# Two staging slots in turn for the split weights of a second product, a slot of its own for the last result of the first MLP, and the split weights reloaded in quarters

## The chip, the cores and the metric

One NeuronCore of a Trainium2 chip runs the whole program. The metric is device time in microseconds (us) of one launch. Three runs of the kernel before gave 925.35, 929.89 and 929.4 us, median 929.4. The profile is of one further execution, 927.71 us, with a span of 926.0 us from its first to its last instruction; the 1.71 us around it are outside the trace.

## The reference

Attention with a causal window of 128 and a linear bias, then two MLPs on 2304 tokens, all in float32:

```python
scores = np.where(mask, scale * q @ k.T + bias, -1e9)      # 4 x 8 heads, 576 tokens, 64 wide
x = softmax(scores) @ v                                    # as 2304 x 512
h = x @ w_in;  x = np.where(h > 0, h, np.exp(np.minimum(h, 0)) - 1) @ w_out     # 512 -> 2048 -> 512
h = x @ w_in2; out = np.maximum(0.01 * h, h) @ w_out2                           # 512 -> 2048 -> 512
```

## The kernel before

Every float32 factor of a matmul is split into a rounded part and its remainder (`hi` by a copy on ScalarE, ACT; `lo` by a subtraction on VectorE, DVE), and each product is three matmuls: hi hi, hi lo, lo hi (`split_mm`).

The first MLP runs over five blocks of tokens `BLK1`, J = 0 to 4, and inside a block over 16 chunks c of 128 hidden units: `mlp1_h` (12 matmuls), activation, and two chunks later `mlp1_y` (12 matmuls) into four PSUM banks y0 to y3. After the last chunk the banks are copied to a tile `ys`, and from there stored to `x2T` in HBM. For J = 4 that is one tile `all_ys` for all four banks.

The second MLP is computed as a 2 x 2 block product with seven products instead of eight. The weights' block sums were made earlier and lie in HBM (`s_in` and `s_out`). Its first half, the 24 units `unit(u)` in three groups of 768 tokens, splits the sums of w_in2 as it goes (`s_load` brings 1,024 KB per pair p into slots w0 to w7, `split_w` splits them). A unit issues its products in the order 1, 5, 4, 6, 3, 2, 7, six matmuls each, where 4 and 3 belong to the unit before; it makes four results, c11, c22, c21 and c12. c11, c22 and c12 lie in turn in three buffers `eg`, c21 and the copy `a` in three buffers `gl`, and `g2_out` stores each to `g2T` in HBM. So c11 of unit u + 1 is written where c11 of unit u was, once its store has landed. The bank of product 2, `pw`, is y0 for an even unit and y1 for an odd one, so unit 0's product 2 waits until y0 has been copied to `ys`.

Its second half, `second(n)`, is 3 x 28 steps of 12 matmuls on results read back from g2T (`raw_load`) and on split weights read from `hlT` (`hl_load`, two tiles of 1,024 KB for each product m).

`hlT` is filled during the 16 chunks of J = 4, one step per chunk: `four_load(n)` reads 512 KB from `s_out` into one of two buffers `wf`, `four_split(n)` splits them with one instruction on ACT (line 301) and one on DVE (line 302) into a tile `hl` of 1,024 KB, and stores that to hlT (line 303). All 16 tiles `hl`, and then `all_ys`, have the one slot "wraw". In the same chunks `s_load` brings the eight tiles s, `x2_load` the first MLP's result for a group (`xr`), and `x2_job` makes the operands of the first products from it.

What sets the order: each engine executes its own queue in order, and so does SyncE's queue (SP), which issues nearly all DMAs. Matmuls, and a few other instructions, are pinned in program order by `keep_in_program_order`; the rest is placed by a list scheduler at build time. A slot of a pool is reused when the last reader of its old tile is done, and a DMA is such a reader until it has landed.

Of the kernel before, what the change touches and what calls it, by code (L numbers as in the profile page):

```python
# [10 lines left out]
F32 = mybir.dt.float32  # L11
F32R = mybir.dt.float32r
# [10 lines left out]
P = 128  # L23
NPAIR = H // 2
NK = DM // P
# [8 lines left out]
HALF = GRP // 2  # L34
NG = NT // GRP
NP2 = NC // 2
# [62 lines left out]
def attention_elu_leaky_kernel(  # L99
# [13 lines left out]
    nc = tc.nc  # L113
# [25 lines left out]
    wp = ctx.enter_context(tc.tile_pool(name="w", bufs=1))  # L139
    wrawp = ctx.enter_context(tc.tile_pool(name="wraw", bufs=1))  # L140
# [116 lines left out]
    hlT = dram.tile([P, 2, 8, NP2, 2 * P], F32, name="hlT")  # L257
# [39 lines left out]
    def four_split(n):  # L297

        src = FOURS.pop(n)
        t = wrawp.tile([P, 2, 4, 2 * P], F32R, tag="wraw", name="hl")  # L300
        nc.scalar.copy(t[:, 0], src)  # L301
        nc.vector.tensor_tensor(t[:, 1], src, t[:, 0].bitcast(F32), op=ALU.subtract)  # L302
        nc.sync.dma_start(out=hlT[:, :, n % 2 * 4:n % 2 * 4 + 4, n // 2], in_=t.bitcast(F32))
# [292 lines left out]
    def mlp1_y(J, cs, gg):  # L596
        gh, gl = gg
        t0, n = BLK1[J]
        per = 512 // n
        if cs[0] == 0:  # L600
            Y[J] = [psp.tile([P, per, n], F32, tag=f"y{i}", name=f"y{i}") for i in range(NK // per)]
        for ci, i, m in [(ci, i, m) for ci in range(len(cs)) for i in range(3) for m in range(NK)]:
            woh, wol = weights(1, cs[ci], 1)
            w, g = ((woh, gh), (woh, gl), (wol, gh))[i]

            matmul(Y[J][m // per][:, m % per, :], w[:, m * P:(m + 1) * P], g[:, ci * n:ci * n + n],
                             start=cs[ci] == 0 and i == 0 and m % per == 0, stop=cs[ci] == NC - 1 and i == 2,
                             skip_group_check=True)
        if cs[-1] == NC - 1:
            if J == len(BLK1) - 1:  # L610

                all_ys = wrawp.tile([P, NK, n], F32, tag="wraw", name="ys")
            for i, y in enumerate(Y.pop(J)):
                if J == len(BLK1) - 1:
                    ys = all_ys[:, i * per:i * per + per]
                else:
                    ys = egp.tile([P, per, n], F32, tag="eg", name="ys")
                if i % 2:
                    nc.vector.tensor_copy(ys, y)  # L619
                else:  # L620
                    nc.scalar.copy(ys, y)  # L621

                q = nc.sync if J < len(BLK1) - 2 or i % 2 else nc.scalar
                q.dma_start(out=x2T[:, i * per:i * per + per, t0:t0 + n], in_=ys)
# [75 lines left out]
    for J in range(len(BLK1) - 1):  # L700
        t0, n = BLK1[J + 1]
# [39 lines left out]
    def s_load(p):  # L741
        t = wp.tile([P, 8, 2 * P], F32, tag=f"w{p}", name="s")
        for o, i, n in ((0, 4, 3), (3, 0, 4), (7, 7, 1)):
            nc.sync.dma_start(out=t[:, o:o + n], in_=sT["in"][:, p, i:i + n])
        S["in", p] = t

    def split_w(u, part):

        s = S["in", u % NP2]
        if part == 2:  # L750
            t = wfp.tile([P, 2, 2, 2 * P], F32R, tag="wf", name="h2")
            hi, lo = t[:, 0], t[:, 1]
            cuts = [(0, 2, 6)]
            H2[u] = hi, lo
        else:
            hi = wp.tile([P, 5, 2 * P], F32R, tag=f"w{8 + u % 2 * 2}", name="h1")
            lo = wp.tile([P, 5, 2 * P], F32R, tag=f"w{9 + u % 2 * 2}", name="l1")
            cuts = [(3, 5, 0), (0, 3, 0)]
            H1[u] = hi, lo
        for a, b, o in cuts:  # L760
            nc.scalar.copy(hi[:, a:b], s[:, a + o:b + o])  # L761
            nc.vector.tensor_tensor(lo[:, a:b], s[:, a + o:b + o], hi[:, a:b].bitcast(F32), op=ALU.subtract)
# [46 lines left out]
        elif n == 6:  # L809
            split("b22", b(1, 1))  # L810

    ps2 = {}

    def product(m, u, bank, start):
        g = u // NP2
        xh, xl = OP[g, OP_OF[m]]
        i = W_OF[m]
        wh, wl = (x[:, i - 6] for x in H2[u]) if i > 5 else (x[:, i] for x in H1[u])
        for kk in range(2):
            s = slice(kk * P, (kk + 1) * P)  # L820
            split_mm(bank, wh[:, s], wl[:, s], xh[:, kk, :], xl[:, kk, :], start and kk == 0, kk == 1,
                     skip_group_check=True)

    def g2_out(u, c, half, tile_, src):
        g, p = divmod(u, NP2)
        nc.scalar.activation(tile_, src, AF.Prelu, alpha=0.01)
        t0 = g * GRP + half * HALF
        nc.sync.dma_start(out=g2T[:, 2 * p + c, t0:t0 + HALF], in_=tile_)

    def small(home, tag, name):  # L830
        return home.tile([P, HALF], F32, tag=tag, name=name)
# [46 lines left out]
    def raw_load(g, role, q, cell):  # L878
        j, k = int(role[1]) - 1, int(role[2]) - 1
        t0, c0 = g * GRP + k * HALF, j * NP2 + 2 * q  # L880
        nc.sync.dma_start(out=cell, in_=g2T[:, c0:c0 + 2, t0:t0 + HALF])
        RAW4.setdefault((g, role), []).append(cell)

    W_HOME = {1: ("w0", "w1"), 5: ("w2", "w3"), 6: ("w4", "w5"), 2: ("w6", "w7"), 7: ("w8", "w9"), 4: ("w12", "w13"),
# [3 lines left out]
    def hl_load(m):  # L888
        A2[m] = [wp.tile([P, NP2, 2 * P], F32R, tag=tg, name="a2") for tg in W_HOME[m]]
        for i in (0, 1):  # L890
            nc.sync.dma_start(out=A2[m][i].bitcast(F32), in_=hlT[:, i, IN_HL[m]])

    def prepare(n):

# [76 lines left out]
    for c in range(NC):  # L971
        g = mlp1_h(J, [c])
        mlp1_y(*pend.pop(0))
        pend.append((J, [c], g))
        if c == 0:
            four_load(0)
        four_load(c + 1)
        four_split(c)
        p = c - 3
        if 0 <= p < NP2:  # L980
            s_load(p)
        if c == 3:
            x2_load(0)
        if 7 <= c <= 13 and c % 2:
            x2_job(0, (c - 7) // 2)
        if c == 14:
            x2_job(0, 4)
            split_w(0, 1)
            split_w(0, 2)
        if c == 15:  # L990
            x2_job(0, 5)
    for x in pend:
        mlp1_y(*x)
        if x is pend[0]:
            x2_job(0, 6)
    split_w(1, 1)

    def raw_cells(role, home, tag, n):
        cells = quarters(home.tile([P, 2 * n, HALF], F32, tag=tag, name="raw"), n)
        for cell in cells:  # L1000
            raw_load(0, role, len(RAW4.get((0, role), ())), cell)

    for u in range(NU):
        g, p = divmod(u, NP2)
# [31 lines left out]
        elif p == 6:  # L1036
            prepare(1)
    hl_load(2)
    raw_cells("b22", wp, "w14", 2)
    hl_load(7)  # L1040
    xb = quarters(x1p.tile([P, 10, HALF], F32R, tag="x1", name="cells"), 5)
    CELLS += [(xb[0], xb[1]), (xb[2], xb[3]), (xa[4], xb[4])]
    prepare(2)
# [3 lines left out]
    for _ in range(2):  # L1047
# [4 lines left out]
    FROM = {"b11": ("b21", (13, 14, 15, 20)), "b12": ("b12", (16, 17, 18, 19)), "b22": ("b11", (21, 22, 23, 24)),  # L1052
            "b21": ("b22", (25, 26, 27, 28))}
    for n in range(NG * len(SEQ)):
        second(n)
        prepare(n + AHEAD)
        g, at_ = divmod(n, len(SEQ))
        for role, (old, when) in FROM.items():
            for q, x in enumerate(when):
                if g + 1 < NG and at_ == x - AHEAD:  # L1060
                    raw_load(g + 1, role, q, RAW4[g, old][q])
# [53 lines left out]
```

## Time and profile before

| | |
|---|---|
| median of three runs | 929.4 us (925.35 to 929.89) |
| profiled execution | 927.71 us, span 926.0 us |
| TensorE (PE) matmul busy | 874.2 us, 94% of the span |
| PE weight loads busy | 769.5 us, 83% |
| DVE busy | 623.1 us, 67% |
| ACT busy | 501.4 us, 54% |
| GpSimd (POOL) busy | 118.9 us, 13% |
| DMA | 169.65 MB, mean 183 GB/s |

Busy shares are means over stages with different limits: attention and the first MLP up to 530 us, the first half of the second MLP from there to 747 us, its second half to the end. A wait costs time only where it holds up the engine that the rest follows, which is PE nearly everywhere. In the rows of waits, "A <- B: total, times, longest" means that A sat idle until B had ended.

### The profile page before, as it was taken

What the parts mean: (1) busy time and instruction counts of PE and PEld (TensorE: products, weight loads), DVE (VectorE), ACT (ScalarE), POOL (GpSimd) and SP (SyncE); (2) the same over time, 40 slices, a digit from 0 to 9 for tenths busy, and PEclk for the clock granted to TensorE, in tenths of its full rate; (3) what the DMA queues carried; (4) which work ended last, traced back from release to release, by engine and by line L of the source; (5) the groups of instructions that cost most, each with busy time, mean ns of one, the idle gap of its engine ahead of it and who ended that gap; (6) DMA issues with size and microseconds to landing.
All of it is one profiled execution on the core that took longest, in us unless ns stands there. A gap on an engine that the chain in (4) does not pass through costs nothing.

```text
span 926.0 us, 14562 instructions
## 1 busy us (share of the span) xinstructions
PE 874.2 (94%) x5077; PEld 769.5 (83%) x5077; DVE 623.1 (67%) x1330; ACT 501.4 (54%) x1067; POOL 118.9 (13%) x281
## 2 busy tenths in 40 slices
PE   8999999999999999999999903999999999999998
PEld 5578878997887877888788703999999999999998
DVE  6799865656767767775845543568676577785953
ACT  7897854445555554554434423667676544444442
POOL 5802222323222221220000000000000000000000
PEclk9999999999999999999999965999999999999999
DMA  9931323224556465345999864345359798527101
GB/s 330 359 131 63 112 91 92 69 69 132 194 177 219 165 225 211 136 186 183 314 317 325 281 236 171 106 151 171 111 188 322 251 343 310 179 66 228 49 1 69
DMA packets 94074, 169.65 MB, mean 183 GB/s; under 512 B 7472, under 2 KB 71216, under 8 KB 92208
## 3 DMA queue, kind: packets, MB, share of 16 engines
q1 hardware_dynamic: 93424, 167.67, 53.4%
q10 hardware_dynamic: 576, 1.05, 0.3%
q8 instruction: 40, 0.66, 0.3%
q14 instruction: 34, 0.28, 0.1%
HBM read 106.82 MB, written 61.87 MB: 182 GB/s over the span
## 4 chain that ended last, share of the span: by engine, by line
PE 75%; DMA 9%; DVE 4%; ACT 3%; issue 1%; ACTq 0%; DVEq 0%
PE px L136 21%; PE h_ps L136 16%; PE y L136 15%; PE pz L136 10%; DMA hlT<-hl 7%; PE pw L136 5%; PE s_ps L136 3%; PE av_ps L136 3%; PE pt_ps L478 2%; ACT hl L301 1%; DVE hl L302 1%; DMA g2T<-c 1%; DMA xr<-x2T 1%; DVE x L790 0%; DVE eg L589 0%
## 5 line engine op out<-in xcount | busy, mean ns | idle before, releaser
L136 PE MATMUL h_ps<-x,w 128*128 128x512 f32 (+1 forms) x960 | 215.0, 373 | 0.9 <-ACT x L127 0.5
L136 PEld LDWEIGHTS h_ps<-x,w 128*128 128x128 f32 x960 | 166.1, 188 | 38.8 <-ACT x L127 4.0
L136 PE MATMUL y<-gh,w 128*128 128x512 f32 (+1 forms) x640 | 157.8, 368 | 1.7 <-DVE ys L619 1.0
L136 PEld LDWEIGHTS y<-gh,w 128*128 128x128 f32 x640 | 113.7, 189 | 22.4 <-DVE ys L619 1.4
L870 ACT CAST cells<-raw 128x768 fp32r<-128x768 f32 x84 | 70.2, 837 | 84.8 <-PE px L136 49.8
L871 DVE TENSOR_TENSOR cells<-raw,cells 128x768 fp32r<-128x768 f32 x84 | 79.1, 953 | 36.8 <-ACT cells L870 36.3
L136 PE MATMUL px<-cells,a 128*128 128x384 f32 x576 | 101.8, 334 | 0.0
L136 PE MATMUL px<-x,h 128*128 128x384 f32 x432 | 99.3, 337 | 2.1 <-ACT b L863 1.7
L136 PEld LDWEIGHTS px<-cells,a 128*128 128x128 f32 x576 | 100.0, 188 | 0.0
L590 ACT CAST gh<-eg 128x512 fp32r<-128x512 f32 (+1 forms) x80 | 46.2, 577 | 77.0 <-DVE eg L589 76.7
L127 ACT ACTIVATE t<-t,stat 128x128 f32<-128x128 f32 (+2 forms) x160 | 62.5, 393 | 43.8 <-DVE t L127 30.1
L127 POOL TENSOR_SCALAR t<-t,stat 128x128 f32<-128x128 f32 (+3 forms) x160 | 71.9, 463 | 91.6 <-DVE stat L127 86.5
L136 PEld LDWEIGHTS px<-x,h 128*128 128x128 f32 x432 | 77.3, 189 | 3.6 <-ACT b L863 2.4
L136 PE MATMUL y<-gl,w 128*128 128x512 f32 (+1 forms) x320 | 78.8, 368 | 0.0
L127 POOL TENSOR_SCALAR_AFFINE_SELECT pt<-pt 128x256 f32<-128x256 f32 (+1 forms) x112 | 45.7, 417 | 213.8 <-ACT pt L490 210.2
L587 ACT ACTIVATE eg<-h_ps 128x512 f32<-128x512 f32 (+1 forms) x80 | 44.0, 550 | 49.2 <-PE h_ps L136 47.9
L591 DVE TENSOR_TENSOR gl<-eg,gh 128x512 fp32r<-128x512 f32 (+1 forms) x80 | 51.2, 639 | 24.7 <-ACT gh L590 24.6
L136 PEld LDWEIGHTS y<-gl,w 128*128 128x128 f32 x320 | 56.9, 189 | 10.0
L761 ACT CAST h<-s 128x512 fp32r<-128x512 f32 (+1 forms) x72 | 49.8, 693 | 28.4 <-PE pz L136 25.0
L136 PE MATMUL pw<-x,h 128*128 128x384 f32 x96 | 25.2, 344 | 37.6 <-ACT ys L621 37.6
L127 DVE CUSTOM_DVE_ANT_0 t<-s_ps,bias 128x256 f32<-128x256 f32 (+4 forms) x160 | 51.6, 369 | 4.5 <-PE s_ps L136 4.0
L136 PE MATMUL pz<-x,h 128*128 128x384 f32 x240 | 53.2, 334 | 0.0
(81 smaller groups left out, 1336.1 us busy)
## 6 DMA issues: line engine op xcount, KB each, us to landing
g2T<-c SPq DMA_DIRECT2D x96, 192.0 KB, 2.2
raw<-g2T SPq DMA_DIRECT2D x48, 384.0 KB, 4.3
wraw<-in_w_in SPq DMA_DIRECT2D x32, 512.0 KB, 4.8
wraw<-in_w_out SPq DMA_DIRECT2D x32, 512.0 KB, 4.9
hlT<-hl SPq DMA_DIRECT2D x16, 1024.0 KB, 5.7
a<-hlT SPq DMA_DIRECT2D x14, 1024.0 KB, 7.7
four<-s_out SPq DMA_DIRECT2D x16, 512.0 KB, 6.5
qkr<-in_kT SPq DMA_DIRECT2D x28, 192.0 KB, 3.3
```

Source lines behind the costliest of these rows:

```text
L127: ins = f(*args, **kw)
L136: tc.keep_in_program_order(nc.tensor.matmul(*args, **kw))
L301: nc.scalar.copy(t[:, 0], src)
L302: nc.vector.tensor_tensor(t[:, 1], src, t[:, 0].bitcast(F32), op=ALU.subtract)
L478: tc.keep_in_program_order(nc.tensor.transpose(ps[:nk, col:col + n], t[:n, c:c + nk], ident[:n, :n]))
L587: nc.scalar.activation(g[:, :m], ps, AF.Exp)
L590: nc.scalar.copy(hi[:, :m], g[:, :m])
L591: nc.vector.tensor_tensor(lo[:, :m], g[:, :m], hi[:, :m].bitcast(F32), op=ALU.subtract)
L761: nc.scalar.copy(hi[:, a:b], s[:, a + o:b + o])
L870: nc.scalar.copy(hi, src)
L871: nc.vector.tensor_tensor(lo, src, hi.bitcast(F32), op=ALU.subtract)
```

## The change

There are five edits. (1) `four_split` stages even steps n in "wraw" as before, and odd steps in "xr" for n under 8, then in turn in w4 (n = 9, 13) and w5 (n = 11, 15). (2) `all_ys` gets the slot w15, which held the last chunk's weights of the first MLP. (3) The loads `s_load` of pairs 0 to 3 come at chunks 4 to 7, of 6 and 7 at chunks 10 and 11, and of 4 and 5 after the last chunk; the first `x2_load` comes at chunk 8 and the operands at 10 to 15. (4) `hl_load` reads quarters of 256 KB, eight for each m, and only queues them; `feed` issues one after each product of a unit, and up to six before each step of the second half. The 16 reads `raw_load` of group 0 are queued likewise, ahead of the quarters. (5) In the last group the stores of the units' results are pinned in program order between those loads.

```diff
@@ -297,7 +297,8 @@
     def four_split(n):
 
         src = FOURS.pop(n)
-        t = wrawp.tile([P, 2, 4, 2 * P], F32R, tag="wraw", name="hl")
+        home, tag = ((wrawp, "wraw") if n % 2 == 0 else (l2, "xr") if n < 8 else (wp, f"w{4 + n // 2 % 2}"))
+        t = home.tile([P, 2, 4, 2 * P], F32R, tag=tag, name="hl")
         nc.scalar.copy(t[:, 0], src)
         nc.vector.tensor_tensor(t[:, 1], src, t[:, 0].bitcast(F32), op=ALU.subtract)
         nc.sync.dma_start(out=hlT[:, :, n % 2 * 4:n % 2 * 4 + 4, n // 2], in_=t.bitcast(F32))
@@ -609,7 +610,7 @@
         if cs[-1] == NC - 1:
             if J == len(BLK1) - 1:
 
-                all_ys = wrawp.tile([P, NK, n], F32, tag="wraw", name="ys")
+                all_ys = wp.tile([P, NK, n], F32, tag="w15", name="ys")
             for i, y in enumerate(Y.pop(J)):
                 if J == len(BLK1) - 1:
                     ys = all_ys[:, i * per:i * per + per]
@@ -809,7 +810,12 @@
         elif n == 6:
             split("b22", b(1, 1))
 
-    ps2 = {}
+    ps2, first, queue = {}, [], []
+
+    def feed(n=1):
+
+        for _ in range(min(n, len(first) + len(queue))):
+            tc.keep_in_program_order((first or queue).pop(0)())
 
     def product(m, u, bank, start):
         g = u // NP2
@@ -820,12 +826,15 @@
             s = slice(kk * P, (kk + 1) * P)
             split_mm(bank, wh[:, s], wl[:, s], xh[:, kk, :], xl[:, kk, :], start and kk == 0, kk == 1,
                      skip_group_check=True)
+        feed()
 
     def g2_out(u, c, half, tile_, src):
         g, p = divmod(u, NP2)
         nc.scalar.activation(tile_, src, AF.Prelu, alpha=0.01)
         t0 = g * GRP + half * HALF
-        nc.sync.dma_start(out=g2T[:, 2 * p + c, t0:t0 + HALF], in_=tile_)
+        store = nc.sync.dma_start(out=g2T[:, 2 * p + c, t0:t0 + HALF], in_=tile_)
+        if g == NG - 1:
+            tc.keep_in_program_order(store)
 
     def small(home, tag, name):
         return home.tile([P, HALF], F32, tag=tag, name=name)
@@ -878,7 +887,13 @@
     def raw_load(g, role, q, cell):
         j, k = int(role[1]) - 1, int(role[2]) - 1
         t0, c0 = g * GRP + k * HALF, j * NP2 + 2 * q
-        nc.sync.dma_start(out=cell, in_=g2T[:, c0:c0 + 2, t0:t0 + HALF])
+        def load():
+            return nc.sync.dma_start(out=cell, in_=g2T[:, c0:c0 + 2, t0:t0 + HALF])
+
+        if g:
+            load()
+        else:
+            first.append(load)
         RAW4.setdefault((g, role), []).append(cell)
 
     W_HOME = {1: ("w0", "w1"), 5: ("w2", "w3"), 6: ("w4", "w5"), 2: ("w6", "w7"), 7: ("w8", "w9"), 4: ("w12", "w13"),
@@ -888,7 +903,9 @@
     def hl_load(m):
         A2[m] = [wp.tile([P, NP2, 2 * P], F32R, tag=tg, name="a2") for tg in W_HOME[m]]
         for i in (0, 1):
-            nc.sync.dma_start(out=A2[m][i].bitcast(F32), in_=hlT[:, i, IN_HL[m]])
+            for q in range(4):
+                to = A2[m][i][:, 2 * q:2 * q + 2].bitcast(F32)
+                queue.append(lambda to=to, i=i, q=q: nc.sync.dma_start(out=to, in_=hlT[:, i, IN_HL[m], 2 * q:2 * q + 2]))
 
     def prepare(n):
 
@@ -976,19 +993,21 @@
             four_load(0)
         four_load(c + 1)
         four_split(c)
-        p = c - 3
-        if 0 <= p < NP2:
-            s_load(p)
-        if c == 3:
+        if 4 <= c < 8:
+            s_load(c - 4)
+        elif c in (10, 11):
+            s_load(c - 4)
+        if c == 8:
             x2_load(0)
-        if 7 <= c <= 13 and c % 2:
-            x2_job(0, (c - 7) // 2)
+        if 10 <= c <= 14:
+            x2_job(0, c - 10)
         if c == 14:
-            x2_job(0, 4)
             split_w(0, 1)
-            split_w(0, 2)
         if c == 15:
             x2_job(0, 5)
+            split_w(0, 2)
+    s_load(4)
+    s_load(5)
     for x in pend:
         mlp1_y(*x)
         if x is pend[0]:
@@ -1036,8 +1055,8 @@
         elif p == 6:
             prepare(1)
     hl_load(2)
+    hl_load(7)
     raw_cells("b22", wp, "w14", 2)
-    hl_load(7)
     xb = quarters(x1p.tile([P, 10, HALF], F32R, tag="x1", name="cells"), 5)
     CELLS += [(xb[0], xb[1]), (xb[2], xb[3]), (xa[4], xb[4])]
     prepare(2)
@@ -1052,6 +1071,7 @@
     FROM = {"b11": ("b21", (13, 14, 15, 20)), "b12": ("b12", (16, 17, 18, 19)), "b22": ("b11", (21, 22, 23, 24)),
             "b21": ("b22", (25, 26, 27, 28))}
     for n in range(NG * len(SEQ)):
+        feed(6)
         second(n)
         prepare(n + AHEAD)
         g, at_ = divmod(n, len(SEQ))
```

What the reordering does shows at three places. First ACT's queue of the kernel before, where the first MLP ends; `hl` is a staging tile (the last three of sixteen splits are here), h2 part of a unit's weights, ys_5661 the last result with y0 the bank of four that unit 0 needs.

```order
L301 CAST hl_5536<-four_5495 128x1024
L301 CAST hl_5578<-four_5534 128x1024
L761 CAST h2_5591<-s_5104 128x512
L301 CAST hl_5627<-four_5576 128x1024
L761 CAST h2_5723<-s_5149 128x512
L621 COPY ys_5661<-y0_5043 128x512
L621 COPY ys_5661<-y2_5045 128x512
L624 DMA x2T_81<-ys_5661 128x512 x2
```

All sixteen splits stand ahead of the copies to `ys`. The same place after the change, with s1, b and c11, c22 the copies and results of units 0 and 1:

```order
L302 CAST hl_5528<-four_5484 128x1024
L622 COPY ys_5661<-y0_5043 128x512
L622 COPY ys_5661<-y2_5045 128x512
L625 DMA x2T_81<-ys_5661 128x512 x2
L849 COPY s1_5685<-px_5676 128x384
L302 CAST hl_5570<-four_5526 128x1024
L762 CAST h2_5623<-s_5143 128x512
L872 COPY b_5717<-px_5676 128x384
L833 ACTIVATE c11_5707<-c11_5707 128x384
L762 CAST h1_5792<-s_5229 128x512
L849 COPY s1_5735<-px_5726 128x384
L302 CAST hl_5616<-four_5568 128x1024
```

The fourteenth split (hl_5528) is now the last ahead of the copies to `ys`; the fifteenth and sixteenth stand among the first two units' work.

Second, SP's queue at the same place, before (the last four staging stores, the stores of `ys`, and the first result of unit 0):

```order
L303 DMA hlT_90<-hl_5497 256x4x256
L294 DMA four_5534<-s_out_89 128x1024
L303 DMA hlT_90<-hl_5536 256x4x256
L294 DMA four_5576<-s_out_89 128x1024
L303 DMA hlT_90<-hl_5578 256x4x256
L303 DMA hlT_90<-hl_5627 256x4x256
L624 DMA x2T_81<-ys_5661 128x512 x2
```

Nothing stands between the last staging store and the stores of `ys`. After the change, from the fourteenth staging store on, with s_5626 and s_5630 the tiles of pairs 4 and 5:

```order
L304 DMA hlT_90<-hl_5528 256x4x256
L294 DMA four_5568<-s_out_89 128x1024
L304 DMA hlT_90<-hl_5570 256x4x256
L745 DMA s_5626<-s_in_88 128x768
L304 DMA hlT_90<-hl_5616 256x4x256
L745 DMA s_5626<-s_in_88 128x1024
L745 DMA s_5626<-s_in_88 128x256
L745 DMA s_5630<-s_in_88 128x768
L745 DMA s_5630<-s_in_88 128x1024
L745 DMA s_5630<-s_in_88 128x256
L625 DMA x2T_81<-ys_5661 128x512 x2
L835 DMA g2T_4929<-c11_5707 128x384
```

Six loads of w_in2's pairs 4 and 5 have moved behind or around the sixteenth staging store (hl_5616), ahead of the first result's store to `g2T`.

Third, DVE's queue in unit 1 before, where c11_5776 and c22_5788 are unit 1's results, a_5833 the copy that unit 2's product 7 waits for:

```order
L859 TENSOR_TENSOR c11_5776<-pw_5728,s1_5735 128x384
L865 TENSOR_TENSOR c22_5788<-pz_5727,b_5786 128x384
L762 TENSOR_TENSOR l1_5868<-s_5235,h1_5867 128x512
L762 TENSOR_TENSOR l1_5868<-s_5235,h1_5867 128x768
L850 COPY a_5833<-px_5801 128x384
```

Two parts of the split of unit 3's weights stand between the results and the copy. After the change:

```order
L763 TENSOR_TENSOR l1_5868<-s_5272,h1_5867 128x768
L868 TENSOR_TENSOR c11_5776<-pw_5728,s1_5735 128x384
L874 TENSOR_TENSOR c22_5788<-pz_5727,b_5786 128x384
L859 COPY a_5833<-px_5801 128x384
L863 TENSOR_TENSOR c12_5841<-pz_5727,a_5758 128x384
```

Those parts have moved ahead of the results, and the copy a_5833 follows them directly.

## Rows read from the trace of the kernel before

**Rows 1.** The page's second part: busy tenths in 40 slices of 23.15 us.

```profile
PE   8999999999999999999999903999999999999998
PEclk9999999999999999999999965999999999999999
DMA  9931323224556465345999864345359798527101
```

**Rows 2.** Waits between 430 and 590 us.

```profile
PE pw L136 <- ACT ys L621: 37.6, 1, 37.6
...
ACT hl L301 <- DMA hlT<-hl: 32.6, 12, 6.9
...
ACT ys L621 <- DMA hlT<-hl: 4.1, 1, 4.1
```

**Rows 3.** Timeline of PE, 420 to 600 us: start, us, engine, line, operation.

```profile
530.07 0.51 PE L136 MATMUL px<-x,h 128*128 128x384 f32 x2
...
533.68 0.34 PE L136 MATMUL px<-x,l 128*128 128x384 f32 x1
571.57 1.01 PE L136 MATMUL pw<-x,h 128*128 128x384 f32 x2 [37.55 <-ACT ys L621]
...
575.34 0.51 PE L136 MATMUL px<-x,h 128*128 128x384 f32 x2
```

**Rows 4.** The chain that ended last, 505 to 580 us: start, us, what.

```profile
506.99 1.06 ACT hl L301
508.07 1.23 DVE hl L302
...
509.32 5.71 DMA hlT<-hl
...
566.16 4.75 DMA hlT<-hl
570.93 0.59 ACT ys L621
```

**Rows 5.** Four stretches: busy time of each engine, granted clock, DMA share, GB/s.

```profile
452.00:520.00 68.00, 68.00 (x301) 56.31 (x301) 38.79 (x56) 27.03 (x39) 0.00 (x0) 1.00 0.95 317
480.00:490.00 10.00, 10.00 (x46) 8.29 (x45) 4.39 (x7) 2.85 (x5) 0.00 (x0) 1.00 0.93 293
530.00:572.00 42.00, 4.08 (x21) 3.41 (x20) 15.65 (x17) 10.30 (x13) 0.00 (x0) 0.59 0.63 214
537.00:538.00 1.00, 0.00 (x0) 0.00 (x0) 0.00 (x0) 0.81 (x1) 0.00 (x0) 0.74 1.09 385
```

**Rows 6.** Timeline of SP's queue, 425 to 600 us.

```profile
434.80 0.32 SPq L294 DMA_DIRECT2D four<-s_out  x1
```

**Rows 7.** DMA issues between 430 and 590 us: KB each, median us to landing.

```profile
hlT<-hl SPq DMA_DIRECT2D x16, 1024.0 KB, 5.7
four<-s_out SPq DMA_DIRECT2D x16, 512.0 KB, 6.5
s<-s_in SPq DMA_DIRECT2D x8, 512.0 KB, 6.2
xr<-x2T SPq DMA_DIRECT2D x2, 1536.0 KB, 8.2
```

**Rows 8.** The chain that ended last, 700 to 735 us.

```profile
714.58 8.45 DMA g2T<-c
...
723.12 0.57 DVE c L859
...
727.05 1.04 PE pz L136 x6
```

**Rows 9.** Waits between 690 and 926 us.

```profile
PE px L136 <- ACT b L863: 1.7, 2, 1.2
```

**Rows 10.** DMA issues between 750 and 926 us.

```profile
raw<-g2T SPq DMA_DIRECT2D x38, 384.0 KB, 4.2
...
a<-hlT SPq DMA_DIRECT2D x4, 1024.0 KB, 12.7
```

## Prediction of the time after the change

> **What bounds the kernel now.** I read four views in turn. The page's slices [rows 1] show PE at 8 to 10 tenths in every slice but the 24th and 25th; there it falls to 0 and 3 tenths, the clock to about half, while DMA is at 9 tenths just before. So the kernel is bound by PE, with one hole. The waits of that stretch [rows 2] name it: product 2 of unit 0 waits 37.6 us, once, for the copy of the bank y0 to `ys` on ACT. PE's timeline [rows 3] gives the place: the first MLP's last matmul is followed by unit 0 at 530.07, the last matmul ahead of the hole ends at 533.68 + 0.34 = 534.02, and the next starts at 571.57, 37.55 us later. The chain [rows 4] says why the copy is late. It is a staircase of equal steps: cast on ACT 1.06, subtraction on DVE 1.23, store of `hl` 5.71, 8.13 us from cast to cast with the gaps. Sixteen tiles in one slot need 16 of these, 130 us. The last store lands at 566.16 + 4.75 = 570.9, so the first cast was at about 441; PE was through with the chunks at 530, and `ys` gets the same slot only at 570.9.
>
> **Is it the slot or the transfers?** In 452 to 520 DMA ran at a share of 0.95 and 317 GB/s [rows 5], that is 317 / 0.95 = 334 GB/s if never idle, and that stretch moved per step 1.05 (hl) + 0.52 (four) + 1.05 (s) = 2.62 MB, 7.8 us at 334. So the staircase and the transfers had nearly the same pace there. In 530 to 572 the share is 0.63 and the rate 214 [rows 5]: there the slot alone set the pace. The change frees the slot, and has the transfers left.
>
> **The wait for `ys`.** After the change ACT's queue holds fourteen casts ahead of the copies to `ys`, not sixteen, and `ys` has a slot (w15) that is free with the last `y` matmul at 530. What can still be late is the fourteenth cast, which needs its 512 KB read. Ahead of the end of that read SP issues 14 reads of 0.524 MB, 12 staging stores of 1.049, six tiles s of 1.049, xr of 1.573 and four stores of an earlier `ys` of 0.262: 7.34 + 12.58 + 6.29 + 1.57 + 1.05 = 28.8 MB (sizes of one of each from [rows 7]), 86 us at 334 GB/s. The first read is issued at 434.80 [rows 6], so 521; a 1 MB store with nothing behind it lands in 4.75 [rows 4], 1.6 over its 3.14 at that rate, so 523; and I add 4 us of idle queue where casts wait in ACT's order between two of PE's chunks: 527. Cast and copy (1.06 + 0.59) then end before or with PE's last y matmul plus a copy, 530.7, and product 2 is due at 534.0. The wait goes, with some 3 us to spare: **minus 37.55**.
>
> With it goes the slow restart. The granted clock fell within 537 to 538 (mean 0.74 there, [rows 5]) after no matmul since 534.0, to half (1.2 GHz), and from 571.57 to 575.34 four groups of three matmuls took 3.77 us [rows 3], at full clock 4 x 0.52 = 2.08 (six take 1.04, [rows 8]): **minus 1.69**.
>
> **What is late next.** Two splits, with their stores, two tiles s and SP's queue behind them move into units 0 to 2. A unit is seven products of 1.04 us [rows 8], 7.28. Unit 0 has five, from 530.07 to 535.7 (0.4 of it allowed for copies that unit 0's own products wait for, **plus 0.4**); unit 1's product 1 ends at 536.7. The sixteenth cast stands behind its copy and some ACT work, so at about 538.2; the store is issued after cast and subtraction, at 540.5, and lands 4.75 later, 545.2 [rows 4]. Then only is w5 free for the last tile s, and SP stands at that load with the stores of `ys` and of every unit's result behind it. 1.05 MB, two stores of 0.26 and the first result of 0.20 are 1.77 MB, 5.3 us at 334, and 1.6 to land: c11 of unit 0 lands at about 552.1. Unit 1's c11 needs that buffer, and on DVE unit 1's c22 and the copy `a` of unit 2 stand right behind it. Three instructions of 0.57 [rows 8] end at 553.8; unit 2's product 7, which needs `a`, is due at 535.7 + 7.28 + 6.24 = 549.2: **plus 4.6**. The trace has this wait in small: at 723.12 a c11 had waited for a store that took 8.45 us behind two 1 MB loads [rows 8], and PE lost 1.2 of it [rows 9]. Bounds: 0, if the stores pass earlier; 9, if the sixteenth split comes 3 us and the store 1.5 us later than that.
>
> A unit later comes the load of xr for the second group, which lay in the hole before. SP now has it behind four more results and ahead of unit 1's c11, whose buffer unit 2's c11 needs: c11 of unit 0 leaves the transfers at 550.5, four results take 2.4, xr 4.7 (1.57 MB), that c11 0.6 and 1.6 to land, 559.8. Three results and copies and one longer subtraction on DVE, some 2.7 us, end with unit 3's `a` at 562.5; its product 7 is due at 549.2 + 4.6 + 1.04 + 6.24 = 561.1: **plus 1.4** (bounds 0 and 3). After unit 4 the queues have caught up. Whether a wait of 4.6 us costs the clock too, no row shows; in the hole it fell within the first 4 us [rows 3, 5], so I take a second slow restart: **plus 1.69** (bounds 0 and 1.69).
>
> **Quarters.** Before, results stored between 1 MB reads waited for these: two waits of product 4 for ACT's copy, 1.7 us in total [rows 9]. With one quarter per product at most 0.26 MB is ahead of a store; **minus 1.7** (bounds: minus 1.7 and plus 3). It is not free: seven quarters and four stores per unit are 1.84 + 0.79 = 2.62 MB in 7.28 us, 360 GB/s against 334, so in the four units with a full feed 0.8 MB, 2.4 us, pile up. A result's buffer is used again after 7.28 us, which covers it. The 42 DMAs more lie on SP, which mostly waits. The quarters of products 2, 7, 4 and 3 (32, 8.39 MB) and six raw reads (2.36 MB) now start only at the second half's first steps: 10.7 MB, 32 us at 334, against a first use after 12 steps of 2.08 = 25 us for the first eight and 56 us for the last. The first eight quarters and the raws are 4.46 MB, 13 us: hidden, 0.
>
> **The sum.** 927.71 - 37.55 - 1.69 + 0.4 + 4.6 + 1.4 + 1.69 - 1.7 = 894.9 for an execution like the profiled one; the same steps from the median of 929.4, 1.7 above it, give 896.6. I predict 895.
>
> **Rivals.** *A, nothing is given back.* The stores are not late, since casts, loads or landings come some 5 us earlier than I put them; against it stands the order on SP, which has the last tile s ahead of all results whatever the speed. 894.9 - 4.6 - 1.4 - 1.69 = 887.
>
> *B, the transfers are the bound.* At 293 GB/s, as in 480 to 490 [rows 5], the 28.8 MB take 98 us; with landing and idle queue the fourteenth cast is at 539, `ys` at 540.7, 6.7 later than product 2 is due. 902. For it: a share of 0.93 in that very stretch. Against: the mean of the 68 us around it is 317.
>
> *C, the change doesn't do what it says.* Two slots, but the same pace, since the transfers and not the slot made the staircase: to end at 571 they would have to run at 28.8 MB / 136 us = 212 GB/s, the rate of the hole. There the share was 0.63 [rows 5], so DMA was waiting, not slow. 928.
>
> *D, slower: the quarters go one at a time.* If each transfer waited for the one before, 32 quarters between 192 and 384 KB (384 KB lands in 4.2 us, [rows 10], so 2.8 for 256 KB) and six raws would take 32 x 2.8 + 6 x 4.2 = 115 us from the start of the second half, 59 later than the last weights are due: 895 + 59 = 954. It makes the kernel slower from 56 + 33 = 89 us on, 2.0 us a quarter. Against it: four reads of 1 MB issued together landed in 12.7 us [rows 10], 330 GB/s, so transfers do overlap.
>
> The Trainium skill speaks for D: its page "DMA: Bandwidth & Descriptors", section "Rules for kernel authors", asks for at least 1 MiB per DMA for full bandwidth, and its section "Bandwidth" gives 341 GB/s at 1 MB and 138 at 64 KB. By the lower figure the 10.7 MB would take 78 us (an estimate from that page), 22 more than there are. For 1 MB the trace agrees (330 GB/s); for 256 KB no run here shows it yet.
>
> **How the numbers follow.** The forecast, some of the hole given back: 0.52. A 0.26, B 0.15, C 0.03, D 0.04. The forecast's own range, from its bounds, is 889 to 901; to leave out no more than 2 in 10, the range must reach into A and B: 884 to 906. A measurement here tells about 0.5% from no change, 4.6 us; forecast, A and B are far beyond it. Faster 0.93, the same 0.03 (C), slower 0.04 (D).
>
> **What would show it.** PE's wait of 37.6 for ACT at `pw` is gone, and the clock is at full to 549. Staging stores overlap: some 5.5 us from cast to cast at first, 8 with the tiles s. DMA's share is over 0.9 until about 548. DVE waits at unit 1's c11 for a store of g2T until about 552, PE some 5 us for DVE's `a` in front of unit 2's product 7. Around 700 the stores land in under 5 us, and PE has no wait there. I am wrong if PE still waits for `ys` over 3 us, if no engine waits for a store near 550, or if PE waits for weights in the second half.

## The result, and the profile after

The changed kernel takes 900.24 us (median of 4 runs, 898.0 to 904.37), beside 928.26 (925.35 to 929.89) of the kernel before on the same chip: a ratio of 0.9706, interval 0.966 to 0.9753. I had predicted 895, range 884 to 906. The profiled execution took 898.99, with a span of 897.3. Line numbers near the splits are one higher than before, those of the units seven to nine (L840 is now L849, L859 L868, L865 L874).

The page's slices, as in [rows 1]: the hole of two slices has shrunk to one slice at 6.

```profile
PE   8999999999999999999989996999999999999998
PEclk9999999999999999999999997999999999999999
DMA  9941323122654646445699799334238999537001
```

PE's timeline, 530 to 563 us, for [rows 3]. Unit 0 starts at 531.70, and its product 2 (`pw`) follows at 535.32 without a wait, its six matmuls in 1.04: the 37.55 us are gone, and with them the slow restart. In their place PE makes one long stop, in front of unit 2's product 3 (`pz`), for 8.37 us. The 15 matmuls from 557.48 to 562.28 then take 4.80 where full clock takes 2.60.

```profile
531.70 0.51 PE L136 MATMUL px<-x,h 128*128 128x384 f32 x2
...
535.32 0.51 PE L136 MATMUL pw<-x,h 128*128 128x384 f32 x2
...
548.77 0.34 PE L136 MATMUL px<-x,l 128*128 128x384 f32 x1
557.48 2.29 PE L136 MATMUL pz<-x,h 128*128 128x384 f32 x6 [8.37 <-DVE c L874]
...
562.28 0.51 PE L136 MATMUL px<-x,h 128*128 128x384 f32 x2
```

The waits of 430 to 590 us, for [rows 2] (total, times, longest). ACT's waits for the store of `hl` are gone. DVE's wait for a store of g2T is behind PE's long wait; the last two rows are a second wait, at 451.74, that I had not foreseen.

```profile
PE pz L136 <- DVE c L874: 8.4, 1, 8.4
DVE c L868 <- DMA g2T<-c: 7.9, 1, 7.9
DVE ys L620 <- DMA x2T<-ys: 5.1, 1, 5.1
...
PE y L136 <- DVE ys L620: 3.4, 1, 3.4
```

The chain behind the long wait, 525 to 560 us, for [rows 4], read downwards: the last read `four`, the 16th cast, its store, SP's issues that stood behind that store, the store of unit 0's c22, DVE, PE.

```profile
532.93 7.51 DMA four<-s_out
...
540.47 1.06 ACT hl L302
...
542.80 5.58 DMA hlT<-hl
...
548.40 0.32 SPq L745
...
551.20 5.65 DMA g2T<-c
...
556.87 0.57 DVE c L874
...
557.48 2.29 PE pz L136 x6
```

The store of unit 0's c11 stands just ahead of that of c22 on SP: it is issued at 550.66, and unit 1's c11 is written into its buffer as soon as it has landed, from 556.24 (next fence). Unit 1's c22 takes the buffer of unit 0's c22 in the same way, 0.6 us later, and PE waits for it.

```profile
556.24 0.56 DVE L868 TENSOR_TENSOR c<-pw,s 128x384 f32<-128x384 f32 x1 [7.89 <-DMA g2T<-c]
```

SP's own timeline, 540 to 563 us, and below it SP's waits of 536 to 560 us. SP first waits 4.4 us for the 16th split itself, whose store it issues at 542.80 (the row names the copy that DVE had just begun behind it). From 543.45 it is at five loads of the last tiles s; the third of them is the first of the last tile, which needs the slot that the 16th split is being stored from, and there SP waits 3.1 us, until 548.40. Two stores of `ys` (copied by 533) and the results (the first ready at 538.7) wait in line behind all this.

```profile
542.80 0.59 SPq L304 DMA_DIRECT2D hlT<-hl  x1
543.45 6.22 SPq L745 DMA_DIRECT2D s<-s_in  x5
549.71 0.91 SPq L625 DMA_DIRECT2D x2T<-ys  x2
550.66 3.78 SPq L835 DMA_DIRECT2D g2T<-c  x5
```

```profile
SPq L304 <- DVE a L859: 4.4, 1, 4.4
...
SPq L745 <- DMA hlT<-hl: 3.8, 2, 3.1
```

Stretches, for [rows 5] (busy time of PE, PEld, DVE, ACT, POOL, then clock, DMA share, GB/s): the transfers run as densely as before up to 520, and through the wait; the clock is at 0.69 of full in the wait and 0.83 behind it, so part of both stretches was at the lower of its two levels, 1.2 GHz.

```profile
452.00:520.00 68.00, 68.00 (x294) 56.09 (x294) 40.37 (x56) 28.69 (x41) 0.00 (x0) 0.97 0.93 313
548.00:558.00 10.00, 1.63 (x8) 1.31 (x8) 1.93 (x4) 1.51 (x3) 0.00 (x0) 0.69 1.01 357
558.00:570.00 12.00, 12.00 (x60) 12.00 (x59) 7.21 (x12) 7.11 (x15) 0.00 (x0) 0.83 0.57 195
```

Waits of 690 to 897 us, for [rows 9]: one of 0.6 us is left of two with 1.7. Of the 18 stores of results issued in 690 to 725, 14 landed in under 5 us, the longest in 6.1.

```profile
PE px L136 <- ACT b L872: 0.6, 1, 0.6
```

PE at the unforeseen wait, in the last block's second chunk. Before, the same matmul waited 1.02 us. From its start to the next group of `y` it takes 6.52 us (451.74 to 458.26), before 4.90 (450.79 to 455.69): 1.62 of slow clock, which is granted at 0.88 of full in 448 to 462.

```profile
451.74 0.50 PE L136 MATMUL y<-gh,w 128*128 128x512 f32 x1 [3.36 <-DVE ys L620]
...
454.85 3.57 PE L136 MATMUL h_ps<-x,w 128*128 128x512 f32 x12
```

### The profile page after: what moved, and what is told of

Same layout as the page of the kernel before. It is cut to its first block, busy times and chain, and to the rows that moved or that the text cites. A ratio compares the mean times of both kernels' runs of the same rounds, so it can differ in the third digit from the quotient of the medians.

```text
span 897.3 us, 14623 instructions
## 1 busy us (share of the span) xinstructions
PE 873.6 (97%) x5077; PEld 769.6 (86%) x5077; DVE 621.7 (69%) x1330; ACT 500.5 (56%) x1067; POOL 118.3 (13%) x281
## 3 DMA queue, kind: packets, MB, share of 16 engines
q10 hardware_dynamic: 576, 1.05, 0.3%
## 4 chain that ended last, share of the span: by engine, by line
PE 86%; DMA 5%; ACT 4%; DVE 3%; issue 1%; POOL 0%; SPq 0%; ACTq 0%; DVEq 0%
PE px L136 21%; PE h_ps L136 20%; PE y L136 20%; PE pz L136 11%; PE pw L136 5%; PE s_ps L136 4%; PE av_ps L136 3%; DMA wraw<-in_w_in 2%; PE pt_ps L479 2%; ACT t L127 1%; DMA four<-s_out 1%; ACT wraw L187 1%; DMA g2T<-c 1%; DMA x2T<-ys 1%; DMA hlT<-hl 1%
## 5 line engine op out<-in xcount | busy, mean ns | idle before, releaser
L589 DVE TENSOR_SCALAR eg<-eg 128x512 f32<-128x512 f32 (+1 forms) x80 | 32.2, 404 | 33.8 <-ACT eg L588 31.8
```

What stands on the lines that cost most here:

```text
L589: nc.vector.tensor_scalar(g[:, :m], g[:, :m], 1.0, -1.0, op0=ALU.min, op1=ALU.add)
```

## The experiments

A kernel's runs differ by some 2 to 8 us, and part of that lies ahead of the changed code. So beside the medians I use two durations from each profile: A, from PE's start on the last block's first chunk (433.81 in the changed kernel) to unit 0, and B, from unit 0 to the span's end.

| kernel | median us | ratio to before, interval | A | B |
|---|---|---|---|---|
| before | 928 to 929 | | 94.87 | 395.93 |
| changed | 900.24 | 0.9706 (0.966 to 0.9753) | 97.89 | 365.60 |
| ys's slot only | 912.98 | 0.9833 (0.9814 to 0.9851) | 94.56 | 382.62 |
| ys back in wraw | 901.14 | 0.9712 (0.9691 to 0.9733) | 96.32 | 368.06 |
| no quarters | 903.17 | 0.9726 (0.9705 to 0.9746) | 99.13 | 368.17 |
| results on ACT's queue | 898.74 | 0.967 (0.9634 to 0.9706) | 98.78 | 363.02 |
| last s later | 892.84 | 0.963 (0.9604 to 0.9656) | 99.73 | 357.38 |
| ACT's queue, xr first | 893.0 | 0.9634 (0.9615 to 0.9653) | 99.19 | 359.81 |
| prior ys in xr | 899.05 | 0.9703 (0.9672 to 0.9733) | 94.55 | 367.68 |
| ACT's queue, xr first, prior ys in xr | 892.41 | 0.9626 (0.9599 to 0.9652) | 94.54 | 364.28 |
| last s later, prior ys in xr | 891.84 | 0.9613 (0.9593 to 0.9633) | 94.51 | 360.40 |
| 40 dummies | 901.07 | 0.971 (0.9692 to 0.9729) | 97.96 | 367.18 |
| 48 dummies | 900.3 | 0.9701 (0.967 to 0.9732) | 98.13 | 365.87 |

**Which part filled the hole?** First the slot of `ys` alone, put into the kernel before:

```diff
-                all_ys = wrawp.tile([P, NK, n], F32, tag="wraw", name="ys")
+                all_ys = wp.tile([P, NK, n], F32, tag="w15", name="ys")
```

> The kernel before with one edit, ys in slot w15; the splits stay in one slot. Theory S (two separate things: the slot holds ys back, and the single staging slot sets the pace of the casts): cast to cast stays at 8.1 us and the 16th cast at about 563; 12 casts stand ahead of the copies to ys on ACT, so these are done at about 532 and unit 0's product 2 does not wait. The last four casts now stand on ACT among the result copies of units 0 and 1, and PE waits for these copies, 13 to 22 us in all at units 1 and 2: 904 to 913 us, 908 likeliest. Rival R1, ys's slot is all that mattered: 895 to 901 us, like the changed kernel or better. Rival R2, the slot of ys alone does nothing since two staging places are what ends the staircase: over 920 us.

912.98, at the upper end of theory S. Unit 0's product 2 no longer waits, but PE stops in unit 1 for 20.21 us (first row: PE; the others: ACT). A cast of weights for unit 0's product 4, which PE works off in unit 1, stands on ACT behind the 15th cast, and that waits 6.92 for a store to leave the only slot. The casts go on to 565.4, as slow as before. I had named the result copies as what is late; it is a cast of weights.

```profile
561.23 3.01 PE L136 MATMUL px<-x,h 128*128 128x384 f32 x8 [20.21 <-ACT h L761]
```

```profile
558.22 1.04 ACT L301 CAST hl<-four 128x1024 fp32r<-128x1024 f32 x1 [6.92 <-DMA hlT<-hl]
560.56 0.62 ACT L761 CAST h<-s 128x512 fp32r<-128x512 f32 x1 [1.29 <-DVE hl L302]
```

And the change without that slot, `ys` put back into wraw in the changed kernel. The second staging place, the moved loads and the quarters all stay; since the odd steps borrow the slots of xr, w4 and w5, staging was not run without the moved loads.

```diff
-                all_ys = wp.tile([P, NK, n], F32, tag="w15", name="ys")
+                all_ys = wrawp.tile([P, NK, n], F32, tag="wraw", name="ys")
```

> The changed kernel with one edit undone: ys in wraw again, behind all 16 casts. Theory S: ys waits for the last store out of wraw (issued at 537.2 in the trace of the changed kernel, some 6 to 8 us to land), so unit 0's product 2, due at 535.3, waits 8 to 12 us with a slow restart behind it; the later wait in front of unit 2's product 3 shrinks from 8.4 to 0 to 2, since the same stores land at the same time and PE now arrives later. So the two waits don't add up: 901 to 906 us. Rival R2, ys's slot does not matter: 900 us within 0.3%. Rival R1, ys's slot is nearly all: 920 us or more.

901.14, as theory S had it. PE waits 8.45 us at unit 0's product 2 instead, and the wait in front of unit 2's product 3 is gone: the same stores land at nearly the same time, and PE meets them once, wherever it comes first. So without `ys`'s own slot the change keeps 27 us of its 28, and the medians don't part. Of the 2.46 by which B is longer, 2.05 come in the second half, where PE waits for ACT (second fence), and ACT had waited 3.40 for an earlier result to be stored; matmul by matmul, the two kernels are 0.5 us apart behind unit 4. A wait at that place also comes, 0.4 to 1.7 us long, in four of the runs below, and its cause was not looked for. The slot by itself is thus worth some 0.5 us here.

```profile
542.71 1.01 PE L136 MATMUL pw<-x,h 128*128 128x384 f32 x2 [8.45 <-ACT ys L622]
```

```profile
779.79 2.52 PE L136 MATMUL px<-cells,a 128*128 128x384 f32 x13 [1.68 <-ACT c L978]
```

**Quarters.** Loads of 1 MB, issued where the program has them:

```diff
-            for q in range(4):
-                to = A2[m][i][:, 2 * q:2 * q + 2].bitcast(F32)
-                queue.append(lambda to=to, i=i, q=q: nc.sync.dma_start(out=to, ...
+            nc.sync.dma_start(out=A2[m][i].bitcast(F32), in_=hlT[:, i, IN_HL[m]])
```

> The changed kernel with the weights' loads of the second half as before: 1 MB each, issued where the program has them, raw reads too, the last stores not pinned. Theory: the waits of product 4 for ACT near 700 to 745 come back, 1.2 to 2.5 us in all, nothing else changes: 901.5 to 903 us. Rival D' (quarters one after the other cost the second half time): faster than the changed kernel, under 899 us. Rival U (quarters are worth more, since the 1 MB reads hold the results' stores up over several units): over 905 us.

903.17: the medians differ by 2.9, with intervals that overlap. In the trace the wait of 0.96 below is back (the later one, 0.57, is in both kernels). From the resumption at `pz` to the end it takes 341.5 us (901.0 - 559.54), the changed kernel 339.8 (897.3 - 557.48): 1.6, the size expected. Start to start, 1.1 of it stand at 699.72, and 0.5 are slow clock right behind the resumption. The rest of the 2.9 lies ahead of it, where the two programs issue the same instructions in the same order.

```profile
699.72 1.66 PE L136 MATMUL px<-x,h 128*128 128x384 f32 x8 [0.96 <-ACT b L870]
```

**What makes the 8.4 us: SP's order or the transfers?** Theory Q has the results' stores held up by their place on SP; rival T by the bytes. First the same stores from another queue:

```diff
-        store = nc.sync.dma_start(out=g2T[:, 2 * p + c, t0:t0 + HALF], in_=tile_)
+        store = (nc.scalar if u < 3 else nc.sync).dma_start(out=g2T[:, 2 * p + c, ...
```

> The changed kernel; the 12 stores of results of units 0 to 2 are issued from ACT's DMA queue, the rest unchanged: same bytes, other queue. Theory Q (the 8.4 us in front of unit 2's product 3 come from SP's order, where the first results' stores stand behind the last split's store and the loads of the last two tiles s): c11 of unit 0 is stored at about 538 to 539 and lands by 546; that wait goes, and the slow clock behind it; ACT pays some 0.4 to 0.6 us for each store, which it has. 889 to 892 us. Rival T (the transfers are the bound there, DMA's share was 1.01 in 548 to 558): the wait only moves, 5 us or more of it stay, 896 to 901 us.

898.74, a miss for Q: I had 889 to 892, and the time can't be told from the changed kernel's. The wait at unit 2's product 3 did go, but another came at 569.42, 3.88 us, with a slow restart, and one of 1.66 at 544.15. ACT stood 4.73 us at a cast of xr, with the copy that PE needs behind it, and xr's load had been issued only at 556.50, behind the tile s that waits for w5. So the head of the line on SP had been moved, not removed (rows of PE and of ACT).

```profile
569.42 1.84 PE L136 MATMUL px<-x,h 128*128 128x384 f32 x8 [3.88 <-ACT b L872]
```

```profile
566.76 0.83 ACT L790 CAST x<-xr 128x768 fp32r<-128x768 f32 x1 [4.73 <-DMA xr<-x2T]
```

So next the loads themselves were moved, with all queues as in the changed kernel:

```diff
-    s_load(4)
-    s_load(5)
...
         unit(u)
+        if u == 1:
+            s_load(4)
+            s_load(5)
```

> The changed kernel; the loads of the last two tiles s moved from the end of the chunks to behind unit 1, so that on SP the stores of unit 0's four results stand ahead of them; queues and bytes as they were. Theory Q (SP's order made the 8.4 us): c11 of unit 0 is stored right behind the last split's store, at about 543.5, and lands by 549; PE's wait in front of unit 2's product 3, due at 549.1, falls to 0 to 2 us. xr of the second group now stands behind more results and lands at 563 to 567; its casts stand on ACT ahead of unit 4's copies, as in the run with results on ACT's queue, and may cost 0 to 5 us there. 890 to 898 us, 893 likeliest. Rival T (the transfers are the bound): 5 us or more of the wait stay in place, 898 to 902 us.

892.84: Q holds. The results are stored right behind the 16th split, from 546.34 (first fence, SP's queue), 0.6 us behind it instead of 7.9 as in the changed kernel (542.80 to 550.66). PE waits 0.84 in place of 8.37 (second fence). The stretch moves nearly the same bytes, only in another order (325 GB/s in 540 to 560, against 335 in the changed kernel), and xr, which I feared for, is in time.

```profile
545.70 0.59 SPq L304 DMA_DIRECT2D hlT<-hl  x1
546.34 4.20 SPq L835 DMA_DIRECT2D g2T<-c  x4
550.59 0.48 SPq L745 DMA_DIRECT2D s<-s_in  x1
```

```profile
552.86 1.31 PE L136 MATMUL pz<-x,h 128*128 128x384 f32 x6 [0.84 <-DVE c L874]
```

The run that had missed, with the last tile s behind xr:

```diff
-    s_load(5)
...
                 x2_load(g + 1)
+                if not g:
+                    s_load(5)
```

> The changed kernel with the results of units 0 to 2 on ACT's DMA queue, as before, and the last tile s loaded behind xr of the second group instead of ahead of it. Theory Q': with the results off SP, the next late thing was xr (issued at 556.5 behind the tile s that waits for the last split's store, landing at 566.7, PE 3.9 us behind it); now SP can issue xr as soon as ys is stored, at about 550, it lands by 560, and no wait over 1.7 us is left in units 0 to 6: 889 to 893 us. Rival T (the bytes set the time, whatever the order): a wait of 3 us or more for xr, for s or for a store comes in its place: 895 to 900 us.

893.0, the upper end of Q'. No wait near 569 is left; one of 1.85 at 544.23 is, a little over the 1.7 that I had allowed, where ACT has the 16th cast and a result ahead of a copy, and one of 1.73 in the second half. xr was issued at 554.54, not 550, and ACT waited 2.5 for it.

```profile
544.23 0.62 PE L136 MATMUL px<-x,h 128*128 128x384 f32 x2 [1.85 <-ACT s L849]
```

**The wait at 451.** DVE's fourth copy of the block before needs the slot of the first, whose store lies behind two stores of `hl` where before there was one. With one tile for that `ys` in slot xr, DVE waits for nothing and the first odd split waits instead:

```diff
+            elif J == len(BLK1) - 2:
+                all_ys = l2.tile([P, NK, n], F32, tag="xr", name="ys")
...
-                if J == len(BLK1) - 1:
+                if J >= len(BLK1) - 2:
```

> The changed kernel; ys of the block before the last is one tile in slot xr instead of four in the small slots, so DVE's fourth copy waits for no store, and the first odd split must wait for ys's stores. The wait of 3.4 us for ys at 451.7 and the slow clock behind it (about 1 us) go. Theory P (what comes later is set by the split's transfers, not by PE): cast 14 and the stores near 545 come no earlier, some 0 to 3 us later; PE reaches units 0 to 2 some 4 us earlier and waits there as much longer, at unit 0's product 2 or unit 2's product 3: 898.5 to 901 us. Rival (the early wait is on the path and adds up): 895 to 897 us.

899.05, which can't be told from the changed kernel. The durations say where the gain went: A falls by 3.34 to 94.55, and B rises by 2.08. PE stops 7.08 us at the same product 3, and in B at five more places for 0.3 to 1.0 us each. Counted from the last block's first chunk, the 16th split is stored at 107.8 us, against 109.0 in the changed kernel: 1.2 earlier, where PE is 3.3 earlier. Theory P has the time about right, and its reason in part. Matmul by matmul, 5.3 us are gained at 451 and behind it; 1.9 come back ahead of unit 0, mostly at 526, where PE waits 1.44 for ACT's `gh`, 1.1 in units 0 to 3, and 1.0 at two places of 699 and 777, far behind the splits. And the edit itself holds the early splits back: the second cast comes 13.4 us behind the chunk's start, where the changed kernel has it at 6.2, and the fourth at 25.8 instead of 22.5. Whether that or the transfers keep the 16th split from coming earlier, no run separates.

```profile
555.34 2.29 PE L136 MATMUL pz<-x,h 128*128 128x384 f32 x6 [7.08 <-DVE c L876]
```

The same edit on top of the two better versions:

> The last kernel together with ys of the block before the last in slot xr. If the two waits add up: 885 to 889 us. If what PE gains at 451 is waited for in units 0 to 4 (theory P), as the run before: 889 to 893 us.

> The changed kernel with both edits, the last two tiles s loaded behind unit 1 and ys of the block before the last in slot xr. With the first alone 892.8 us were measured, with the second alone 899.05. Theory P (PE's gain at 451 runs into the split's transfers, since they set when unit 0's results can be stored): the wait at 451 goes, but 1 to 3 us come back at units 0 to 4: 890 to 893 us. Rival (nothing waits there any more, so all of it shows): 887 to 889 us.

892.41 and 891.84. In the first A falls by 4.65 and B rises by 4.47; in the second by 5.22 and 3.02. Both times lie in P's range: of some 5 us, 0.2 and 2.2 are kept. The second is the fastest kernel here, and its interval (0.9593 to 0.9633) lies wholly below that of the changed kernel (0.966 to 0.9753). Its wait at product 3 is 1.17.

**Does the wait cost the clock too?** Dummy matmuls in front of unit 2's product 3, in the changed kernel; 40, and 48 in a second run:

```diff
+        if u == 2:
+            d = psp.tile([P, HALF], F32, tag="y2", name="dummy")
+            for _ in range(40):
+                matmul(d, H1[u][0][:, 0, :P], OP[0, "b11"][0][:, 0, :], start=True, stop=True)
```

> The changed kernel with 40 matmuls of 128x384, whose result nobody reads, put on PE in front of unit 2's product 3, where PE waited 8.4 us: 40 x 0.174 = 7.0 us of work in the wait, so PE stands still for 1 to 2 us instead. Theory C (the wait costs the clock too): the clock stays at full, the groups of six matmuls behind the wait take 1.04 to 1.3 us instead of 2.3, 1.9 and 2.3, and the time falls by 2 to 3 us: 897 to 898.5 us. Rival (the longer matmuls behind the wait have another reason): the groups stay at 1.9 to 2.3 us and the time at 900 us.

> The changed kernel with 48 matmuls that nobody reads in front of unit 2's product 3. With 40 of them 1.9 us of waiting were left and the matmuls behind it were still slow (six in 2.0 and 1.9 us). 48 take 8.4 us and leave 0.3 to 1 us. Theory C: behind a wait as short as this the clock stays at full, the groups of six take 1.04 to 1.35 us, the stretch 558 to 570 has a mean clock of 0.98 or more, and the time is 1 to 2.5 us below the changed kernel's 900.2: 897.5 to 899.5. Rival (slow matmuls come from something else in that stretch, such as the transfers): still 1.9 to 2.3 us for six, a mean clock under 0.95, 900 us or more.

With 40, PE still waited 1.89 us and the six behind took 2.02, so it told nothing; 901.07. With 48 nothing is left to wait for at that place, the clock is at full throughout 548 to 570, and the six take 1.33: the slow matmuls do come from PE's standing still, not from the transfers. But the time is 900.3, unchanged, and there theory C was wrong. Matmul by matmul, 2.1 us are gained behind the wait and 1.0 come back at the next unit's product 3, which waits 0.72 (first fence; the third is the stretch 558 to 570). There DVE waits 1.19 at unit 2's c11 for the store of unit 1's c11 (second fence), which SP had issued at 559.77, behind the load of xr (556.87). Another 1.2 come back at copies near 683 and 706, for a reason that was not looked for.

```profile
559.81 1.33 PE L136 MATMUL pz<-x,h 128*128 128x384 f32 x6
...
568.11 1.33 PE L136 MATMUL pz<-x,h 128*128 128x384 f32 x6 [0.72 <-DVE c L878]
```

```profile
567.01 0.56 DVE L872 TENSOR_TENSOR c<-pw,s 128x384 f32<-128x384 f32 x1 [1.19 <-DMA g2T<-c]
```

```profile
558.00:570.00 12.00, 11.14 (x63) 10.50 (x62) 7.54 (x12) 6.94 (x13) 0.00 (x0) 1.00 0.73 250
```

## Why the prediction was right, and where not

The mechanism came as forecast: the hole goes, and a smaller wait, for the stores of unit 0's results, takes its place. Step by step, in us:

| step | predicted | measured |
|---|---|---|
| the wait for ys | -37.55 | -37.55 |
| slow restart behind it | -1.69 | -1.69 |
| small waits in unit 0 | +0.4 | 0.20, against 0.36 before |
| wait for c11's store (c11's and c22's) | +4.6 | +8.37 |
| load of xr | +1.4 | 0 |
| second slow restart | +1.69 | +2.20 |
| waits near 724 and 745 | -1.7 | 1.74 to 0.57, so -1.17 |
| wait for the prior block's ys | not foreseen | +2.34, and +1.62 of slow clock |

From unit 0 on these sum to -30.0, and B fell by 30.33. In A the last row, less the 0.63 (and 0.28 of slower matmuls) that PE lost before at 527 and no longer does, makes +3.05; A rose by 3.02. Ahead of A nothing was changed, and this execution was 1.39 earlier: -28.7 in all, from 927.71 to 898.99. That this is only 4.1 above the sum of 894.9 is in part luck: what came later than forecast adds up to 7.8 us, and what came earlier to 3.7.

**The mis-sized term** is the wait for c11's store. Its chain was right, link by link, and three of its numbers were not. The place: I had PE stop at unit 2's product 7, for `a`. It stops at product 3, two products earlier, since that one adds into a bank that c22 of unit 1 must first read; by my own times that makes 553.2 - 547.1 = 6.1. The landings: the 14th cast was at 529.92, not 527; the last read `four` took 7.51 in a full queue; the last split's store was issued at 542.80, not 540.5, and took 5.58, not 4.75; c22's, by which PE was held, took 5.65, behind 2.8 us of SP's issues (c11's 5.6, behind 2.3). So DVE was through with c22 at 557.4 and not 553.2, +4.2. And PE came 2 us later than I had it, which took 2.0 off: 6.1 + 4.2 - 2.0 = 8.3. I had put queueing into the rate of the transfers, but took landing times for single stores from calmer stretches [rows 4].

**The load of xr** cost nothing here, but its step was not wrong. With the clock kept at full by 48 dummies, PE came to unit 3 earlier and met just that wait, 0.72 us for DVE behind the store that stands behind xr; in the changed kernel the slow clock, 2.2 us, hid it.

**What I did not see** is the wait at 451.74. I had counted the stores of that earlier `ys` as bytes only. With a second staging place, two stores of `hl` lie ahead of them instead of one, and a buffer of three comes free later. So the clock was not at full to 549 either, as I had it among the signs.

**The rivals.** A (nothing given back, 887) is wrong: the store was late by more than I had it. B (the transfers are the bound, 902) has the time nearly right and the reason wrong: its wait for `ys` is not there, and the run with the last tiles s moved takes 8.2 us off the duration from unit 0 on, with nearly the same bytes. The transfers still bear on when the 16th split can be stored: its read took 7.51 us, and their share was 0.94 in 530 to 549. C (the same pace, 928) is out: ACT waits for no store of `hl` any more. For D, quarters one at a time, no wait for weights appears in the second half. In 700 to 750, 44 quarters landed in 5.4 us each at the median (below), while the core's transfers moved 350 GB/s at a share of 0.98. The Trainium skill's page "DMA: Bandwidth & Descriptors", section "Rules for kernel authors", asks for at least 1 MiB per DMA for maximum bandwidth; with many queued, 256 KB was enough here.

```profile
a<-hlT SPq DMA_DIRECT2D x44, 256.0 KB, 5.4
```

## What to carry to other kernels

When a wait on a slot goes, follow the queue that issued into that slot: everything in line behind a DMA that waits for its buffer waits too, and here moving the loads of two tiles behind four small stores gave back 7 of the 8 us. Price the new wait by landing times from the busiest stretch, and look for every reader of the bank, not only for the value that is produced last. Time gained ahead of a stretch with dense transfers may come back behind it, as more than half of it did in three runs here; compare two durations from the trace, one on either side, before calling it a gain, and look where inside them the time is lost.

## What the runs showed that I had not expected

Taking stores off SP's queue removed the wait of 8.37 us from its place, though in that run DMA was at a share of 1.05 and 380 GB/s in 540 to 550; the total moved only once xr stood ahead of the last tile s as well. The Trainium skill's page "DMA: Bandwidth & Descriptors", section "Rules for kernel authors", says that spreading DMAs over issuing engines only saves the sequencer's issue time. As to bandwidth the run agrees: 341 GB/s in 540 to 560, against 335 in the changed kernel, and the 16th split's store took 10.57 us to land instead of 5.58. What the second queue saved was not issue time but the wait of a load at the head of SP's line.

The clock did not follow the length of a short wait alone: behind 1.89 us (40 dummies) six matmuls took 2.02 us, behind 1.85 us (ACT's queue, xr first) the clock stayed at 1.00 through 540 to 550. Plainer still is the wait for the prior block's `ys`, ahead of which the changed kernel and the one with `ys` back in wraw issue the same instructions. It lasted 3.36 us in the one, with a clock of 0.88 in 448 to 462, and 3.37 in the other, with a clock of 1.00 in the same stretch. So A of single executions differs by 1.6 us from this alone. What else decides it, these runs leave open.
